# Attention and gated feed-forward on one core: constant copies moved in ScalarE's order, row maxima added first, a new list of steps

## The chip, the cores and the metric

The program runs on one core of a Trainium2 chip. The metric is the device time of one execution in microseconds (us), lower is better. The kernel before takes 883.32 us (median of 3 runs, 883.28 to 883.49).

## The reference

Eight batches, eight heads, 576 positions, head size 64. Heads 0 to 3 attend to the 32 nearest earlier positions; heads 4 to 7 to every fourth of the last 128. What comes out (4608 tokens of 512 numbers) goes through a gated feed-forward layer.

```python
scores = scale * np.matmul(q, k.transpose(0, 1, 3, 2))          # scale = 1/sqrt(64)
mask_plain = (rel >= 0) & (rel < 32)
mask_dil = (rel >= 0) & (rel < 128) & (rel % 4 == 0)
scores = np.where(masks[None], scores, -1e9)
scores = scores - np.max(scores, axis=-1, keepdims=True)
attn = np.exp(scores)
attn = attn / (np.sum(attn, axis=-1, keepdims=True) + 1e-09)
out = np.matmul(attn, v)                    # q: [8, 8, 576, 64]
x = out.transpose(0, 2, 1, 3).reshape(4608, 512)
h = x @ w_in                                # w_in: 512 x 2048
g = h * np.tanh(log1p(exp(h)))
return g @ w_out                            # w_out: 2048 x 512
```

## The kernel before, in words

The work is cut into 16 units, each half of a batch (288 tokens). Of each unit the attention is done for four pairs of heads, then the first product with `w_in` (`ff1`), the gate, and the second product with `w_out` (`ff2`). Every number is held as a high and a low 16-bit part, so a product with weights is three 16-bit products. Units 0 to 2 ("direct") do their attention in f32 and take the plain weights; from unit 4 on the first product is done with seven combined forms of the weights for two units at once.

The weights themselves are made on the chip, in pieces `(k, g, p)` (k = 0 for `w_in`, 1 for `w_out`; g a chunk of 512 columns, p a half of its rows). A piece goes through steps with names of two letters: `wl` loads it into one of four buffers `raw`, `wm` takes a magnitude on ScalarE (L392/L394), `ww` shifts that and joins it to the raw words on VectorE (L445, L447), `wa` takes absolute values on ScalarE (L399), `ws` sums magnitudes over partitions on TensorE (L413) and makes a scale on VectorE (L420 to L426), `wp` splits into a high part on ScalarE (L458) and a low part on VectorE (L461). The raw buffer is free for the next load after that.

Attention of a direct unit `u` and pair: `sp` puts mask and scores into a PSUM bank (L683: the identity copy `ident_b` times the mask copy `m_fb`; L686: q times k); `sc` takes the negated maximum of each row on VectorE (L716, into `nm`). Units 0 and 1 (`ACROSS`) then make the scores a second time, transposed, in `across` (step `tp`): masks, k times q, and `nm` times the identity in f32 are added up in one bank (three loops, all L819), and ScalarE takes the exponential from there (L839). Unit 2 transposes its probabilities instead (L800). `va` multiplies with the values (L853), `tx` transposes the result (L897 with `is_transpose`, L900) and takes away the high part (L915). `pr` makes the scale of a unit's values (magnitudes L350 on ScalarE, `largest`: L355 on TensorE, L358 and L360 on VectorE, L363 on TensorE).

All steps are generators. `ORDER`, a list of some 2,350 names that a planner wrote out, sets which generator is advanced next; `=n` behind a name gives the number of the buffer that the step takes. Each engine carries out its instructions in that order. `kwN` (`keep_warm`) issues N products of a 128x128 tile of zeros on TensorE (L1169); nobody reads what they give.

Three copies of constants on ScalarE stand outside the list: `m_fb` (L294), `ident_b` (L296), `minus` (L315). A scheduler places these; on ScalarE they stand behind the first `wm` (L392). The loads of a unit (`loads`, L475 to L496) are issued on SP's queue; those of unit 0 are in two parts, with a `yield` between.

Of the kernel before, what the change touches and what calls it, by code (L numbers as in the profile page):

```python
# [43 lines left out]
wl0.0.0=1 wm0.0.0=0 ww0.0.1 kw4=1 kw4=2 kw4=3 kw4=1 sp0.0=2 kw4=3 kw4=1 kw4=3 sc0.1 tp0.1=0 kw4=1 xa1.1=0 kw4=3
ww0.0.1 ww0.0.0 kw4=1 ww0.0.0 kw4=1 kw8=3 wa0.0.1 wa0.0.0 kw4=1 kw4=3 tp0.1=1 kw4=1 sc0.0 ws0.0=1 ws0.0 kw4=3 ld0
sp0.2=2 wl0.3.0=2 tp0.0=0 sc0.2 tp0.2=3 kw4=1 wm0.3.0=0 ww0.3.0 xa0.0=1 lv0 va0.1=2 ww0.3.0 pr0=0 kw12=1 wl0.3.1=3
kw4=1 wp0.0.1 xa2.1=2 pr0=1 wp0.0.1 pr0 lv1 tp0.0=0 ld1 wl0.2.0=0 tp0.2=1 sp0.3=0 sc0.3 xa1.0=3 wm0.3.1=0 pr0=3 pr0
ww0.3.1 kw4=1 va0.0=1 wp0.0.0 kw4=0 ww0.3.1 kw4=3 kw4=0 kw4=3 va0.1 tp0.3=0 va0.0 kw12=3 wa0.3.0 kw4=3 wa0.3.1 ws0.3=3
xa0.1=4 va0.0=0 kw4=1 tp0.3=0 va0.3=0 va0.3 wp0.0.0 wl0.2.1=1 va0.2=1 va0.1=2 ws0.3 wp0.3.0 tx0.0=3 va0.3=1 kw4=2
tx0.0 wp0.3.0 va0.2 wp0.3.1 sp1.1=0 va0.2=3 sp1.0=2 sc1.1 wp0.3.1 tx0.0 tx0.0 wm0.2.0=0 sc1.0 tx0.1=1 tx0.1 sp1.2=0  # L50
sc1.2 wm0.2.1=0 ww0.2.0 ww0.2.0 ww0.2.1 wl0.1.1=2 ww0.2.1 tp1.0=3 tx0.1 tx0.1 tp1.2=2 sp1.3=0 ff0.6=1 tp1.0=0 ff0.7=3
wa0.2.0 wm0.1.1=0 sc1.3 ww0.1.1 wa0.2.1 wl0.1.0=3 ws0.2=0 wm0.1.0=0 pr1=1 ff0.6 ww0.1.0 ws0.2 ws0.1=0 ff0.7 ws0.1
pr1=0 pr1 tp1.2=1 ff0.0=2 pr1=0 wp0.2.1 wp0.2.1 pr1 fs0 wp0.2.0 wp0.2.0 ff0.0 tp1.3=0 ff0.6=1 ww0.1.0 fs1 va1.0=1
ff0.0=2 ff0.7 wl1.2.0=1 va1.2=2 tp1.3=0 ff0.1=3 wl1.2.1=0 va1.3=0 ff0.1 va1.0 va1.2 ww0.1.1 va1.0=0 va1.2=2 tp1.1=1
wp0.1.0 wp0.1.0 wm1.2.0 ww1.2.0 wp0.1.1 wp0.1.1 tp1.1=0 ff0.4=2 va1.3 va1.3=3 ff0.4 tx1.1=1 wm1.2.1 ww1.2.1 ww1.2.1
va1.1=0 ld2 ff0.1 ff0.4=0 ws1.2=3 gt0.0=0 va1.1 ff0.5=2 wl1.3.1=3 ws1.2 va1.1=1 tx1.1 gt0.0 ww1.2.0 gt0.3=1 ff0.5
ff0.5 gt0.2=2 gt0.2 ff0.3=3 tx1.0=2 tx1.0 wm1.3.1 tx1.1 wp1.2.0 wp1.2.0 ff0.2=0 ff0.2 tx1.1 lv2 pr2 ff0.2=2 ff0.3
ff0.3 tx1.0 tx1.0 sp2.3=1 sp2.1=0 ff1.2=3 wl1.3.0=2 ff1.2 sc2.3=0 ff1.6=2 ff1.6 wm1.3.0 gt0.3 sc2.1=1 ww1.3.1 wp1.2.1
ex2.1 ww1.3.0 ex2.3 ff1.6=0 wp1.2.1 ww1.3.1 ws1.3=0 ww1.3.0 ws1.3 ff1.2=1 ff1.3=1 gt0.1=7 gt0.1 wl1.0.0=1 ff1.3 ff1.3
ff1.7=2 pr2=0 wm1.0.0 tp2.3=1 lv3 tp2.3=1 sp2.0=3 wp1.3.0 ff1.7 wl1.0.1=0 pr2 fo0.2.0=1 fo0.2.1 tp2.1=0 ff1.7 sp2.2=2  # L60
wf1.1=2 wm1.0.1 wp1.3.0 ww1.0.0 wp1.3.1 wf1.1 sc2.2=2 sc2.0=1 gt1.1=3 fo0.3.0 tp2.1=0 ex2.0 wl1.1.1=2 ex2.2 fo0.3.1
gt1.1 ff1.1=0 ff1.1 va2.1=3 ww1.0.1 fs2 va2.3=2 wp1.3.1 wl1.1.0=3 ww1.0.1 va2.1 va2.3 va2.1=0 va2.3=3 wf1.1=1 wf1.1
fo0.2.2 tp2.2=3 wm1.1.1 ww1.1.1 ws1.0=2 ws1.0 tp2.2=0 fo0.2.3 wf1.1 gt1.3=4 va2.2=3 va2.2 ff1.0=2 wm1.1.0 gt1.3 ff1.0
xa3.1=1 ff1.0=2 va2.2=1 ff1.1 gt1.0=5 ww1.1.0 fo0.3.2 fo0.3.3 fo0.3.3=0 fo0.2.3=1 fo0.3.3 ww1.1.0 tx2.1=3 tx2.1
tp2.0=2 tp2.0=1 ww1.1.1 ld3 wp1.0.1 ww1.0.0 wp1.0.0 ff1.5=0 ff1.5 wp1.0.1 ws1.1=1 ws1.1 ff1.4=2 tx2.1 tx2.1 wp1.1.1
ff1.4 ff1.4=0 va2.0=1 va2.0 wp1.1.0 wp1.0.0 fo0.0.0=3 fo0.0.1 fo0.0.2 gt1.0 fo1.2.0=2 fo1.2.1 wf0.0=1 ff1.5 wp1.1.1
fo0.2.3 fo1.3.0 fo0.0.3 va2.0=2 wp1.1.0 gt1.2=6 wf1.0=2 tx2.0=0 gt1.2 ol pr3 pr3 wf0.0 wf1.0 pr3 pr3=1 pr3 fo1.2.2
# [1162 lines left out]
```

## Time and profile before

| | |
|---|---|
| median of 3 runs | 883.32 us |
| the profiled execution | 883.64 us |
| its span | 881.9 us |
| TensorE (PE) busy | 867.8 us, 98% of the span |
| VectorE (DVE) busy | 668.4 us, 76% |
| ScalarE (ACT) busy | 676.0 us, 77% |
| products of zeros (L1169) | 208 |

The span runs from the first to the last instruction; the execution's own time is 1.74 us more. The page of the profile gives each engine's busy time over the whole span, and TensorE is busy nearly throughout. So the questions are in which stretches it is idle or slow, and which of its instructions need not be there. The views used are the busy times by stretch, with the clock that TensorE was granted (1.00 is 2.4 GHz, 0.50 is 1.2 GHz), the waits of TensorE, and the timelines of the first 130 us.

### The profile page before, as it was taken

Reading aid. Unit: us, or ns where it says so; the run is one execution under the profiler, and the core shown is the slowest. Engines: PE = TensorE matmul, PEld = TensorE weight load, DVE = VectorE, ACT = ScalarE, POOL = GpSimd, SP = SyncE. Lnnn points to the kernel's source line nnn. Section 1 sums busy time; section 2 is a strip of 40 time slices with the busy share of each in tenths; the row PEclk is TensorE's granted clock in tenths of the full one; section 3 lists DMA queues with packets and bytes.
Section 4 is the critical chain, followed back from the end, with each engine's and each line's share of the span. In section 5 each row is a group of like instructions: output and inputs, shape, how many; then the busy total and the mean of one; then the engine's idle time right before and its main releaser. Section 6 shows DMA issues by size and latency. Waiting matters only on the chain.

```text
span 881.9 us, 21715 instructions
## 1 busy us (share of the span) xinstructions
PE 867.8 (98%) x9076; PEld 700.9 (79%) x9079; DVE 668.4 (76%) x1034; ACT 676.0 (77%) x978; POOL 19.0 (2%) x93
## 2 busy tenths in 40 slices
...
GB/s 253 219 114 240 154 139 96 126 163 169 148 174 185 201 198 190 168 159 179 211 154 189 174 155 213 167 163 218 168 155 180 117 194 111 121 117 159 111 8 48
DMA packets 211010, 141.21 MB, mean 160 GB/s; under 512 B 151392, under 2 KB 195936, under 8 KB 210912
## 3 DMA queue, kind: packets, MB, share of 16 engines
...
## 4 chain that ended last, share of the span: by engine, by line
PE 65%; DVE 6%; ACT 4%; issue 1%; DMA 1%; DVEq 0%; ACTq 0%
PE b L1140 33%; PE b L1025 26%; PE b L859 3%; PE b L686 2%; DVE nm L716 1%; DVE sb L710 1%; DVE g L1130 1%; DMA w<-wd 1%; PE b L1113 1%; DVE p L790 1%; ACT sb L743 0%; ACT L743 0%; DVE hm L971 0%; DVE w L1010 0%; DVE g L1010 0%
## 5 line engine op out<-in xcount | busy, mean ns | idle before, releaser
L1140 PE MATMUL b<-g,w 128*128 128x288 f16 x3072 | 391.9, 286 | 1.2 <-DVE w L461 1.2
L1140 PEld LDWEIGHTS <-w 128*128 128x128 f16 x3072 | 296.4, 98 | 75.8 <-DVE w L461 1.4
L1025 PEld LDWEIGHTS <-w 128*128 128x128 f16 x2016 | 195.3, 98 | 50.0 <-DMA w<-wd 0.4
L1025 PE MATMUL b<-xf,w 128*128 128x288 f16 x1440 | 211.1, 286 | 0.1
L1130 DVE SCALAR_TENSOR_TENSOR g<-hm,sg,g 128x1152 f16<-128x1152 f32 x64 | 90.1, 1411 | 29.1 <-ACT g L1128 29.0
L1113 PE MATMUL b<-xf,w 128*128 128x288 f16 x768 | 99.6, 286 | 0.4 <-DVE y L1152 0.2
L1113 PEld LDWEIGHTS <-w 128*128 128x128 f16 x768 | 74.3, 98 | 20.0 <-issue 0.6
L1128 ACT ACTIVATE g<-hm,sg 128x1152 f16<-128x1152 f32 x64 | 80.0, 1252 | 1.1
L1154 ACT ACTIVATE y<-b,fo 128x288 f32<-128x288 f32 x60 | 42.7, 736 | 41.1 <-PE b L1140 41.1
L1035 ACT ACTIVATE hm<-hm,fs 128x576 f32<-128x576 f32 x72 | 54.1, 768 | 13.3 <-DVE hm L1086 8.6
L1025 PE MATMUL b<-w,w 128*128 128x288 f16 x288 | 63.4, 286 | 0.0
L743 ACT ACTIVATE sb<-sb,ln_p 96x768 f32<-96x768 f32 (+3 forms) x52 | 46.3, 897 | 9.0 <-DVE sb L718 8.8
L718 DVE TENSOR_TENSOR sb<-sb,nm 96x768 f32<-96x768 f32 (+4 forms) x64 | 49.2, 769 | 2.2
L716 DVE TENSOR_REDUCE nm<-sb 96x6 f32<-96x768 f32 (+4 forms) x64 | 48.8, 763 | 1.8
L790 DVE TENSOR_TENSOR p<-sb,p 96x768 f16<-96x768 f32 (+3 forms) x52 | 46.8, 904 | 2.9 <-ACT p L788 2.9
L1086 DVE TENSOR_TENSOR hm<-b,hm 128x576 f32<-128x576 f32 x24 | 18.1, 753 | 38.8 <-PE b L1025 33.8
...
L859 PEld LDWEIGHTS <-pT 128*128 128x128 f16 (+3 forms) x1092 | 38.5, 98 | 2.2
L1025 PE MATMUL b<-xg,w 128*128 128x288 f16 x288 | 39.2, 286 | 0.2 <-ACT hm L1042 0.2
L1010 DVE TENSOR_TENSOR w<-w,w 72x1024 f16<-72x1024 f32 (+3 forms) x31 | 29.6, 957 | 6.6 <-ACT w L1008 6.6
L686 PEld LDWEIGHTS <-q 64*72 64x72 f16 (+1 forms) x1092 | 27.8, 116 | 8.4 <-issue 8.1
L1008 ACT CAST w<-w 72x1024 f16<-72x1024 f32 (+3 forms) x31 | 25.8, 836 | 10.5 <-DVE w L999 2.7
...
## 6 DMA issues: line engine op xcount, KB each, us to landing
...
```

Source lines behind the costliest of these rows:

```text
L686: nc.tensor.matmul(o, q, k, start=start, stop=stop, skip_group_check=True)
L716: nc.vector.tensor_reduce(nm[:nq, :, j:j + n], x, axis=AX.X, op=ALU.max, negate=True)
L718: nc.vector.tensor_tensor(blocked(sb, c0, n, w), x, nm[:nq, :, j:j + n].unsqueeze(3).broadcast_to([nq, 2, n, w]), op=ALU.add)
L743: nc.scalar.activation(x, x, AF.Exp, bias=ln_p[:nq])
L790: nc.vector.tensor_tensor(lo, src, hi, op=ALU.subtract)
L859: nc.tensor.matmul(avv[:, h, j], pp[:nk, c:c + P], vv[vi][:nk, j, hh, :], start=(i == 0), stop=(i == 2))
L1025: nc.tensor.matmul(o[:, h, :HT], t[:, c, wi, h * P:(h + 1) * P], form_of(p, x, c, xi), skip_group_check=True, start=start and n == 0, stop ...
L1035: nc.scalar.activation(o, src, AF.Mish, scale=U[2 * p]["fs"][:, j:j + 1])
L1113: nc.tensor.matmul(ph[:, h, :HT], w1[j][c // WIDE][:, c % WIDE, wi, k * P:(k + 1) * P], x_of(d, xi, c), start=(n == 0), stop=(n == len(seq ...
L1128: nc.scalar.activation(g[:, 0], m, AF.Identity, scale=sg)
L1130: nc.vector.scalar_tensor_tensor(g[:, 1], m, sg, g[:, 0], ALU.mult, ALU.subtract)
L1140: nc.tensor.matmul(po[:, :HT], w2[:, e, j, wi, k * P:(k + 1) * P], d["g"][j][:, gi, k, :], start=(j == 0 and n == 0), stop=(j == NCH - 1 a ...
```

## The change

1. The three copies on ScalarE are issued at the head of the list, behind the first activation.
2. In `across` the product with `nm` comes first, with `is_transpose=True`; it opens the accumulation (`start`), and the last product of q and k closes it.
3. `ORDER` is another list: the same steps, each as often as before, in another order up to about a third of the list, then in the same order with a few other buffer numbers. The 45 `kw` entries with 208 products of zeros become 35 with 164. The loads of unit 0 are in two parts in both kernels; `loads` is not touched.

```diff
@@ constants
     m_fb = const.tile([QB, 2 * P + QB], BF16, name="m_fb")
-    nc.scalar.mul(m_fb, m_f, math.sqrt(D))
     ident_b = const.tile([QB, QB], BF16, name="ident_b")
-    nc.scalar.copy(ident_b, ident[:QB, :QB])
...
     minus = const.tile([P, P], F16, name="minus")
-    nc.scalar.mul(minus, ident, -1.0)
@@ across
+        for j, x in enumerate(bl):
+            for h in range(2):
+                mm(at(h, x), nm[:nq, h, j:j + 1].broadcast_to([nq, x[2]]), ident[:nq, :nq], is_transpose=True, start=j == 0,
+                   stop=False)
         for x in bl:
             for h in range(2):
-                mm(at(h, x), m_fb[:nq, col:col + x[2]], ident_b[:nq, :nq], start=x is bl[0], stop=False)
+                mm(at(h, x), m_fb[:nq, col:col + x[2]], ident_b[:nq, :nq], start=False, stop=False)
...
-                mm(at(h, x), kn[hs, k0:k0 + x[2]], d["qn"][hs, pair, x[1]:x[1] + nq], start=False, stop=False)
-        for j, x in enumerate(bl):
-            for h in range(2):
-                mm(at(h, x), nm[:nq, h, j:j + 1].broadcast_to([nq, x[2]]), ident[:nq, :nq], start=False, stop=x is bl[-1])
+                mm(at(h, x), kn[hs, k0:k0 + x[2]], d["qn"][hs, pair, x[1]:x[1] + nq], start=False, stop=x is bl[-1])
@@ the list is carried out
         nc.scalar.activation(first, ln_p, AF.Exp)
+        nc.scalar.copy(ident_b, ident[:QB, :QB])
+        nc.scalar.mul(m_fb, m_f, math.sqrt(D))
+        nc.scalar.mul(minus, ident, -1.0)
@@ ORDER
-kw4=0 kw8=1 kw4=0 kw4=2 kw4=3 kw4=0 kw4=2 kw4=1 kw4=3 kw8=0 kw4=1 kw4=2 kw4=3 ld0 sp0.1=0 wl0.0.1=0 wm0.0.1=0 kw4=1
...
+kw4=3 kw4=0 kw4=1 kw4=2 kw8=3 kw4=0 ld0 wl0.0.1=0 kw4=1 wm0.0.1=0 ww0.0.1 ww0.0.1 kw4=2 kw4=3 kw4=1 kw4=3 kw4=2 xa1.1=0 kw8=0 kw4=1 kw4=3 sp0.1=2 sp0.0=0
...
```

ScalarE at the start of the program, before (first fence) and after the change (second). `raw_76` and `raw_77` are the first two loaded pieces of `w_in`, `w_...` their places.

```order
L1179 ACT_TABLE_LOAD
L1179 ACTIVATE first<-ln_p 128x1
L392 ACTIVATE w_119<-raw_76 128x1024
L296 CAST ident_b<-ident 96x96
L315 ACTIVATE minus<-ident 128x128
L294 ACTIVATE m_fb<-m_f 96x352
L392 ACTIVATE w_118<-raw_77 128x1024
```

```order
L1177 ACT_TABLE_LOAD
L1177 ACTIVATE first<-ln_p 128x1
L1178 CAST ident_b<-ident 96x96
L1179 ACTIVATE m_fb<-m_f 96x352
L1180 ACTIVATE minus<-ident 128x128
L389 ACTIVATE w_116<-raw_76 128x1024
L389 ACTIVATE w_115<-raw_77 128x1024
```

The three copies have moved from behind the first magnitude, which reads a loaded piece, to ahead of it.

VectorE at the start of the program, before and after; `nm` are the row maxima of the first two pairs.

```order
L445 TENSOR_SCALAR w_119<-w_119 128x1024
L716 TENSOR_REDUCE nm<-b_72 96x2x2
L716 TENSOR_REDUCE nm<-b_72 96x2
L447 SCALAR_TENSOR_TENSOR raw_76<-raw_76,w_119 128x1024
L445 TENSOR_SCALAR w_118<-w_118 128x1024
L447 SCALAR_TENSOR_TENSOR raw_77<-raw_77,w_118 128x1024
L716 TENSOR_REDUCE nm<-b_74 96x2x2
```

```order
L442 TENSOR_SCALAR w_116<-w_116 128x1024
L444 SCALAR_TENSOR_TENSOR raw_76<-raw_76,w_116 128x1024
L713 TENSOR_REDUCE nm<-b_74 96x2x2
L713 TENSOR_REDUCE nm<-b_74 96x2
L442 TENSOR_SCALAR w_115<-w_115 128x1024
L444 SCALAR_TENSOR_TENSOR raw_77<-raw_77,w_115 128x1024
L713 TENSOR_REDUCE nm<-b_72 96x2x2
```

The joining of the first piece now stands ahead of the first row maxima.

TensorE at the first `across` (step `tp0.1`), before and after; rows that repeat are left out, x4 is a number of products.

```order
L1169 MATMUL b_75<-zeros 128x128
L819 LDWEIGHTS m_fb
L819 MATMUL b_72<-ident_b,m_fb 128x96
L819 MATMUL b_72<-ident_b,m_fb 96x96
L819 MATMUL b_72<-qn,knp 128x96 x4
L819 MATMUL b_72<-qn,knp 96x96 x2
L819 MATMUL b_72<-ident,nm 128x96 x4
L819 MATMUL b_72<-ident,nm 96x96 x2
```

```order
L1167 MATMUL b_75<-zeros 128x128
L816 MATMUL b_73<-ident,nm 128x96 x4
L816 MATMUL b_73<-ident,nm 96x96 x2
L816 LDWEIGHTS m_fb
L816 MATMUL b_73<-ident_b,m_fb 128x96
L816 MATMUL b_73<-ident_b,m_fb 96x96
L816 MATMUL b_73<-qn,knp 128x96 x4
L816 MATMUL b_73<-qn,knp 96x96 x2
```

The products with `nm` went from the end of the step to its head.

## Rows read from the trace of the kernel before

**Rows 1.** Busy time by stretch: stretch, its us, engines' busy us (instructions), PEclk, DMA share, GB/s.

```profile
1.05:6.06 5.01, 5.01 (x60) 4.83 (x60) 0.00 (x0) 1.17 (x2) 2.40 (x14) 1.00 0.77 206
6.06:11.33 5.27, 0.00 (x1) 0.12 (x1) 0.69 (x1) 1.87 (x4) 0.00 (x0) 0.97 0.99 365
11.33:17.50 6.17, 6.17 (x48) 4.96 (x47) 3.91 (x5) 2.27 (x2) 0.00 (x0) 0.50 1.08 309
17.50:53.97 36.47, 36.36 (x512) 31.87 (x513) 23.91 (x44) 24.40 (x33) 0.78 (x2) 1.00 0.72 210
53.97:143.20 89.23, 87.75 (x858) 72.44 (x857) 79.67 (x142) 74.36 (x119) 2.97 (x2) 1.00 0.52 159
143.20:299.00 155.80, 153.53 (x1694) 122.76 (x1694) 150.66 (x240) 135.19 (x198) 8.91 (x31) 1.00 0.64 151
299.00:870.00 571.00, 570.70 (x5854) 457.55 (x5849) 409.36 (x601) 434.50 (x622) 3.45 (x39) 1.00 0.63 158
```

**Rows 2.** TensorE's waits: who waited for whom, us in total, times, longest.

```profile
PE b L683 <- ACT m_fb L294: 5.3, 1, 5.3
PE b L355 <- ACT vdh L350: 1.7, 1, 1.7
PE b L1140 <- DVE w L461: 1.2, 1, 1.2
```

**Rows 3.** ScalarE's timeline: start us, us, line, operation, tiles, count, idle before.

```profile
9.40 1.12 ACT L392 ACTIVATE w<-raw 128x1024 f32<-128x1024 f32 x1 [7.18 <-DMA raw<-in_w_in]
10.79 0.48 ACT L294 ACTIVATE m_fb<-m_f 96x352 bf16<-96x352 f32 x1
11.87 1.12 ACT L392 ACTIVATE w<-raw 128x1024 f32<-128x1024 f32 x1 [0.60 <-DMA raw<-in_w_in]
15.66 1.15 ACT L399 ACTIVATE w<-raw 128x1024 bf16<-128x1024 f32 x1 [2.67 <-DVE raw L447]
23.67 1.06 ACT L350 ACTIVATE pp<-vdn 72x1024 bf16<-72x1024 f32 x1
```

**Rows 4.** VectorE's timeline, the first row maxima and the first pieces of weights.

```profile
10.56 0.69 DVE L445 TENSOR_SCALAR w<-w 128x1024 int32<-128x1024 int32 x1 [9.57 <-ACT w L392]
13.55 0.95 DVE L716 TENSOR_REDUCE nm<-b 96x4 f32<-96x512 f32 x2 [2.29 <-PE b L686]
14.42 1.21 DVE L447 SCALAR_TENSOR_TENSOR raw<-raw,w 128x1024 int32<-128x1024 int32 x1
17.80 0.95 DVE L716 TENSOR_REDUCE nm<-b 96x4 f32<-96x512 f32 x2 [0.31 <-PE b L686]
```

**Rows 5.** TensorE's timeline from the first scores to the first `ff1`.

```profile
11.33 0.75 PE L683 MATMUL b<-m_fb,ident_b 96*96 96x352 bf16 x2 [5.27 <-ACT m_fb L294]
12.01 1.49 PE L686 MATMUL b<-knp,qn 64*96 64x128 f32 x12
...
18.43 0.43 PE L819 MATMUL b<-ident_b,m_fb 96*128 96x96 bf16 x6
18.79 0.86 PE L819 MATMUL b<-qn,knp 64*128 64x96 f32 x12
19.58 1.47 PE L819 MATMUL b<-ident,nm 96*128 96x96 f32 x12
20.88 2.17 PE L1169 MATMUL b<-zeros 128*128 128x128 f16 x36
22.89 1.03 PE L413 MATMUL b<-w,ones 128*128 128x512 bf16 x3
...
28.50 1.26 PE L819 MATMUL b<-ident,nm 72*72 72x72 f32 x16
...
38.15 1.03 PE L413 MATMUL b<-w,ones 128*128 128x512 bf16 x3
...
47.86 1.58 PE L819 MATMUL b<-ident,nm 96*128 96x96 f32 x12
...
51.13 1.68 PE L819 MATMUL b<-ident,nm 72*104 72x72 f32 x16
...
53.97 3.11 PE L1113 MATMUL b<-xf,w 128*128 128x288 f16 x24
```

**Rows 6.** TensorE's timeline, transposes of 96x96 (six) and 72x72 (eight) tiles.

```profile
86.17 0.66 PE L897 MATMUL b<-ident,xs 96*128 96x96 f32 x6
105.69 0.69 PE L800 MATMUL b<-ident,sb 72*72 72x72 f32 x8
```

**Rows 7.** VectorE's timeline, L421 early and while GpSimd clears buffers.

```profile
24.68 0.15 DVE L421 TENSOR_SCALAR wf<-wm 128x1 int32<-128x1 int32 x1
...
139.18 1.25 DVE L421 TENSOR_SCALAR wf<-wm 128x4 int32<-128x4 int32 x1
```

More of the change, by code (lines that the diff above doesn't have):

```diff
@@ L42 @@
 ORDER = """
-kw4=0 kw8=1 kw4=0 kw4=2 kw4=3 kw4=0 kw4=2 kw4=1 kw4=3 kw8=0 kw4=1 kw4=2 kw4=3 ld0 sp0.1=0 wl0.0.1=0 wm0.0.1=0 kw4=1
[L44 to L67, printed above, removed]
@@ new lines @@
+xa1.1=0 kw8=0 kw4=1 kw4=3 sp0.1=2 sp0.0=0 kw4=1 sc0.1 kw4=3 kw4=1 wl0.0.0=1 wm0.0.0=0 ww0.0.0 kw4=3 ww0.0.0 kw4=1
+kw8=3 tp0.1=1 ld0 sp0.2=3 wa0.0.1 kw4=2 wl0.3.0=2 kw4=2 wa0.0.0 lv0 wm0.3.0=0 sc0.0 ws0.0=0 kw4=2 wl0.3.1=3 sc0.2
+tp0.2=3 tp0.1=0 pr0=1 ws0.0 kw4=2 va0.1=0 ww0.3.0 ww0.3.0 tp0.0=1 wp0.0.1 wp0.0.1 tp0.0=0 tp0.2=1 kw8=2 sp0.3=2 kw4=1
+pr0=1 kw8=3 wa0.3.0 kw4=3 xa0.0=1 pr0 pr0=1 wm0.3.1=0 va0.0=3 sc0.3 kw4=2 lv1 pr0 kw4=1 ww0.3.1 va0.1 wp0.0.0 ww0.3.1
+ld1 tp0.3=2 wp0.0.0 va0.0 kw4=1 wa0.3.1 kw8=1 ws0.3=1 tp0.3=0 va0.0=0 va0.1=2 va0.3=2 tx0.0=0 ws0.3 xa0.1=2 va0.3
@@ new lines @@
+wp0.3.0 va0.2=1 kw4=3 wl0.2.0=0 kw4=3 va0.2 tx0.0 sp1.1=3 tx0.0 va0.3=0 wp0.3.1 wp0.3.0 va0.2=1 sp1.0=2 sc1.1 tx0.1=1
+sp1.2=3 sc1.0 tp1.0=2 tx0.0 wp0.3.1 wl0.2.1=1 wm0.2.0=0 sc1.2 tx0.1 ww0.2.0 ww0.2.0 wm0.2.1=0 tx0.1 tx0.1 ww0.2.1
+wl0.1.1=2 wa0.2.0 ww0.2.1 tp1.0=1 wa0.2.1 wm0.1.1=0 wl0.1.0=3 tp1.2=0 lv2 sp1.3=3 wm0.1.0=0 sc1.3 ff0.6=1 xa1.0=3
+ws0.2=2 ws0.2 ww0.1.0 ff0.7=3 ff0.7 pr1=0 ww0.1.1 ws0.1=2 ff0.6 tp1.2=0 ws0.1 pr1=0 pr1 ff0.0=2 wp0.2.0 wp0.2.1 pr1=0
+wp0.2.0 ff0.0 pr1 fs0 ff0.6=0 ff0.7 va1.2=0 ff0.0=1 va1.0=1 wl1.2.0=0 va1.0 va1.2 wp0.2.1 tp1.3=3 tp1.3=1 ff0.1=2
@@ new lines @@
+ww0.1.1 wp0.1.1 va1.0=1 wl1.2.1=1 va1.2=3 ww0.1.0 wm1.2.0 wp0.1.1 tp1.1=3 ww1.2.0 tp1.1=0 wp0.1.0 wp0.1.0 ld2 va1.3=1
+ff0.1 va1.3 va1.1=0 fs1 wm1.2.1 ff0.4=3 va1.3=2 ff0.4 va1.1 wl1.3.1=2 ff0.1 gt0.3=4 ww1.2.1 ff0.4=2 va1.1=0 ws1.2=1
+tx1.0=0 ww1.2.1 tx1.0 ws1.2 tx1.1=2 ff0.5=3 ww1.2.0 gt0.3 ff0.5 tx1.1 tx1.1 gt0.0=3 tx1.0 wl1.3.0=3 pr2 ff0.2=1 ff0.5
+tx1.1 ff0.2 ff0.3=3 xa3.0=4 ff0.3 wp1.2.0 wp1.2.0 tx1.0 wp1.2.1 wp1.2.1 sp2.3=2 wm1.3.0 ww1.3.0 gt0.0 sp2.1=0 ff0.2=0
+ff0.3 wl1.0.0=0 sc2.3=0 sc2.1=1 wm1.3.1 gt0.2=0 ff1.2=1 ff1.6=3 ff1.6 ex2.3 ff1.2 ww1.3.1 ws1.3=2 wl1.1.1=1 ww1.3.0
@@ new lines @@
+ex2.1 ff1.7=0 ff1.7 gt0.2 ff1.2=1 ff1.6=2 ws1.3 gt0.1=2 wp1.3.0 tp2.3=2 ww1.3.1 sp2.2=1 ff1.7 wp1.3.0 ff1.3=3 gt0.1
+sc2.2=3 ff1.3 tp2.3=1 wf1.1=0 xa2.1=1 pr2=0 pr2 wm1.0.0 ww1.0.0 wf1.1 fo0.2.0=2 wm1.1.1 ww1.1.1 fo0.2.1 sp2.0=0 ff1.3
+ex2.2 fo0.2.2 sc2.0=2 wl1.0.1=3 wm1.0.1 wp1.3.1 ww1.0.1 tp2.1=3 tp2.1=0 fo0.3.0 va2.3=1 ex2.0 wp1.3.1 ww1.0.1 fo0.3.1
+tp2.2=3 gt1.1=1 gt1.1 tp2.2=1 va2.1=0 ws1.0=3 va2.1 va2.3 va2.1=1 fo0.3.2 gt1.3=5 fo0.3.3 fo0.3.3=1 ws1.0 wp1.0.1
+wf1.1=1 ww1.0.0 va2.2=0 va2.2 fo0.2.3 ld3 ff1.0=3 ff1.0 gt1.3 wl1.1.0=2 wm1.1.0 va2.3=0 ff1.1=1 va2.2=3 ff1.0=2 fs2
@@ new lines @@
+ww1.1.0 wp1.0.0 ws1.1=0 tx2.1=3 ff1.1 fo0.2.3=0 ww1.1.1 ww1.1.0 tx2.1 xa2.0=2 ws1.1 ff1.1 gt1.0=6 ff1.5=2 tx2.1 wf1.1
+tx2.1 ff1.4=1 ff1.4 wp1.0.0 fo0.0.0=0 tp2.0=3 wp1.1.1 wp1.1.0 tp2.0=1 wp1.1.1 wp1.1.0 wf1.1 ff1.5 va2.0=3 ff1.4=0
+ff1.5 gt1.2=7 gt1.0 lv3 wp1.0.1 fo0.0.1 fo0.0.2 wf0.0=2 gt1.2 va2.0 fo0.0.3 va2.0=3 tx2.0=2 ol pr3 pr3 fo0.2.3
+fo1.2.0=1 fo1.2.1 wf1.0=0 pr3 pr3=3 wf0.0 fo0.0.3=0 mr fo0.3.3 wf1.0 fo0.0.3 fo1.2.2 pr3 pr3=3 wf0.0=1 wf0.0 pr3
+fo1.2.3 pr3 fo0.1.0 xw3.0=1 wf0.1=2 pr3 pr3 wf0.0 fo1.2.3=1 fo1.2.3 pr3 pr3 ld4 fo0.1.1 fo0.1.2 fo0.1.3 pr3 tx2.0
@@ new lines @@
+zc2.0 tp6.1=0 za2.1=2 za2.1=2 zl2.6=2 zb2.1=3 zl2.7=0 tp6.1 tp6.2 zb2.1=0 fo3.1.3=0 zd2.1 zc2.1 zg2.1 zl2.8=1 va6.0=1
+pr7 tp6.1=0 gt4.0=1 gt4.0 zd2.1 zg2.1 pr7 pr7 ze2.1 ze2.1 za2.2=3 va6.0 zf2.1 zc2.2=0 pr7 pr7 zc2.1 za2.2=1 zc2.2
+zf2.1 gt4.1=2 va6.0 pr7 gt4.1 zb2.2=2 zb2.2=2 sp7.0=0 va6.1=1 sc7.0=3 va6.1 zl2.9=2 va6.1 zd2.2 zg2.2 zd2.2 ze2.2
+zl2.10=0 ze2.2 zc2.2 za2.3=0 ze2.1 tp6.3=0 tp6.3 zg2.2 zg2.1 gt5.1=5 gt5.1 zf2.2 zf2.2 sp7.1=1 zl2.11=1 tp6.2=1
+zc2.3=2 za2.3=0 zc2.3 gt4.2=4 gt4.2 zl2.12=2 zg2.2 zb2.3=3 sc7.1=0 zd2.3 sp7.2=2 sc7.2=2 zl2.13=0 ze2.2 zt3.0.0=0
```

223 lines of the change are left out of this document (109 added, 114 removed).

## The prediction

> **What bounds the kernel now.** The busy times by stretch come first. From 17.5 us to 870 us TensorE is idle for only 0.11 + 1.48 + 2.27 + 0.30 = 4.2 us [rows 1], so time can come only from its own instructions, its clock, or the stretch before. That stretch is poor: 5.27 us of idle, then 6.17 us at the granted clock 0.50, which is 1.2 GHz [rows 1]. The waits name the cause of the idle: the first mask product waits 5.3 us for `m_fb` [rows 2]. ScalarE's timeline shows why `m_fb` is late: it stands behind the magnitude of the first piece of weights, which starts at 9.40 when the load lands [rows 3]. VectorE is the second engine to watch: from 143.2 to 299 us it is busy 150.66 of 155.80 us [rows 1], so a lead of TensorE can't be spent there freely.
>
> **1. The copies of constants.** In the new order they wait for no load, only for the mask that GpSimd builds, and GpSimd's work is over by 6.06 [rows 1]; so they end far ahead of 9.40. The last of them ended at 11.27 before, so the second magnitude could be thought to start sooner; it doesn't, because it waited for its load until 11.87 anyway [rows 3]. The order on SP's queue is unchanged through the loads of unit 1, so I let the loads land when they did.
>
> What then starts the chain? The list puts the shift and the joining of the first piece ahead of the first row maxima on VectorE. From 9.40: magnitude 1.12 [rows 3], shift 0.69, joining 1.21, maxima 0.95 [rows 4], together 13.4 us. TensorE is there earlier: 68 zeros instead of 60 end at about 6.5, two pairs of scores cost 2.2 us each even at the low clock [rows 5], and 28 zeros cost 1.6. That is 12.6 at worst, and near 10.5 at the full clock if q and k have landed. These were issued ahead of the piece that landed at 9.40, so they take the start at most to 9.4 + 2.2 + 1.6 = 13.2. Either way `tp0.1` starts at 13.4 instead of 18.43 [rows 5]: **5.0 us gained**. The half-clock stretch is inside this number.
>
> The change adds a wait here: the product with `nm` now leads its step, so masks and q-times-k products, 0.43 + 0.86 us [rows 5], queue behind it, and ScalarE's exponential behind those. Before, they ran while VectorE finished: maxima ready at 18.75, needed at 19.58 [rows 4, 5]. In `tp0.1` this wait is in the 13.4; in the later steps the maxima are earlier in the order, and I price it at nothing. If that cover went, it would be up to 1.2 us a step.
>
> **2. From `tp0.1` to the first `ff1`.** Before, this took 53.97 - 18.43 = 35.54 us [rows 5], with 0.11 idle. Three terms change it.
> - *Zeros*: 112 stood here, 68 do now. At 36 in 22.89 - 20.88 = 2.01 us one costs 0.056 [rows 5]; 44 fewer are **2.5 us**.
> - *Row maxima as transposes*: six products in f32 show as 12 instructions of together 1.47 us; six transposes of the same size show as 6, and take 0.66 [rows 5, 6]. The forms here: two steps of 96 rows in unit 0 (1.47 - 0.66 = 0.81 each), two of 72 rows (1.26 - 0.69 = 0.57 each), and in unit 1 `tp1.0` (1.58 - 0.66 = 0.92) and `tp1.2` (1.68 - 0.69 = 0.99). Together **4.7 us**.
> - *New waits*: TensorE alone would now need 35.54 - 0.11 - 2.5 - 4.7 = 28.2 us and be at `ff1` at 41.6. VectorE has some 24 us of work in the old stretch [rows 1] and would have to do it in 28, so it will end last now and then. Following the order with the durations above I find two places. The small product behind `pr0` comes about 0.7 us after TensorE, since VectorE first splits the first piece. The weight sum of chunk 3 (at 38.15 before) waits for ScalarE's absolute values of its second piece, which wait for shift and joining, 0.69 + 1.21 + 1.15 [rows 3, 4]; I get 29.8 against TensorE at 29.1. I take **1.6 us lost** as an estimate. Bounds: 0, and 4.5 if the values of unit 0 land only when ScalarE read them before, at 23.67 [rows 3]; I count on about 21.
>
> So `ff1` starts at 43.2 instead of 53.97.
>
> **3. After the first `ff1`.** Two more `across` steps, `tp1.1` and `tp1.3`: 0.92 + 0.99; four zeros: 0.2. Together **2.1 us**. All other TensorE work is the same, in another order up to some 300 us and in the old order after. Its 4.05 us of idle there [rows 1] I leave as they are, which is the nearest row. Bounds: all of it gone, or 5 us more, since VectorE's own idle in the dense stretch is 5.1 us and TensorE's lead could be lost there. Other buffer numbers in the last two thirds I price at nothing: that stretch has 0.30 us of idle in 571 [rows 1].
>
> **The sum.** 5.0 + 0.1 + 2.5 + 4.7 - 1.6 + 2.1 = 12.8. From the profiled execution's 883.64 that is 870.8; the median of the runs lies 0.3 below it, so **870.5 us**.
>
> A rule bears on the second term. Rows show the transposes at 0.66 of 1.47, a factor of 0.45. The Trainium skill, "TensorE: Matmul & The Clock Gate" (Terms), gives the transpose mode as four times faster for FP32. By that the eight steps would save about 8 us where the rows give 6.6, and the time would be 869. The rows are the same operation in the same program, and decide.
>
> **Rivals.**
> - *The hand-over is rebuilt worse.* Between units 1 and 3 TensorE already waits 1.7 us for magnitudes and 1.2 us for a split [rows 2], and VectorE is slow there while GpSimd clears buffers: the same small operation took 1.25 us there and 0.15 at another time [rows 7]. If the new list lays these clearings on other VectorE work, some 5 us come on top: 875.5. For it: VectorE's 97% in that stretch. Against it: the engine's work up to each weight split is nearly the same in both lists.
> - *The clock falls in the wait before `tp0.1`.* If q and k land early, TensorE idles up to 2.9 us there. The clock fell during the 5.27 us of idle at 6.06, and did not in the waits of 1.7 and 1.2 us [rows 1, 2]; this one lies between. It came back after 6.17 us of work [rows 1]. Half of that is 3.1 us: 873.5.
> - *The start gains nothing*, because loads, not `m_fb`, hold the first scores until 11.33. Then the copies don't do what they are moved for, and 5.0 us are missing: 875.5. Against it: after `m_fb` the scores followed without any wait [rows 5].
> - *Slower: the clock stays low through the heads of unit 0.* With 44 zeros fewer and 112 product instructions turned into 56 transposes, TensorE might stay at 0.50 from 13.4 to the first `ff1`. That adds up to 28 us: near 898. It decides once the low clock lasts for some 25 us, since half of that eats the 12.8. Against it: 48 products, spaced by no more than their own length, brought the clock back in 6.17 us [rows 1], and the new stretch has as dense a stream. The Trainium skill, "TensorE: Matmul & The Clock Gate" (Part 4), says that transposes don't count towards the full clock as products do; no run here shows it, as the longest row of transposes is 0.69 us between products [rows 6].
>
> **How the numbers follow.** A measurement of this kernel can tell about 0.2% (1.8 us) from no change: under 881.5 is faster, over 885.1 slower. Forecast 0.63, worse hand-over 0.14, clock in the wait 0.11, no gain at the start 0.06, low clock throughout 0.04, and 0.02 for gains eaten up to nothing. All but the last two are faster: 0.94; same 0.02; slower 0.04. The range: from 870.5 down by the 4.05 us of idle and half of the waits, 866; up by the worse hand-over and most of the waits' bound, 878. It takes in the second to fourth cases.
>
> **What would show it.** Right, if in the new profile the first mask product starts before 9.4 us without a wait for `m_fb`; if the first transposes of `nm` start near 13.4, in groups of 6 and 8 at 0.66 and 0.69 us; if the first `ff1` starts at 43 (42 to 46); if TensorE is busy some 855 us; and if the stretch behind it, up to the end, is some 826 us long. Wrong, if TensorE's idle between 43 and 290 us is over 8 us, if the granted clock is 0.50 behind 13.4, or if `nm` still shows two instructions for a product.

## The result, and the profile after

The changed kernel takes **870.15 us** (median of 4 runs, 868.49 to 870.64) against 883.40 us for the kernel before (median of 4 runs, 883.28 to 884.84). The ratio is 0.9843, with a 95% interval from 0.9826 to 0.9860: 13.25 us less, where 12.8 were forecast. The profiled execution took 870.22 us; its span is 868.4 us, 13.5 less than before. TensorE is busy for 858.3 us of it (99%).

Busy time of the changed kernel by stretch, columns as in [rows 1]. The stretches end where TensorE's work changes: zeros; first scores; the wait ahead of `tp0.1`; up to the first `ff1`; and then up to the same distance from the end as in [rows 1].

```profile
1.05:6.79 5.74, 5.74 (x68) 5.74 (x69) 0.00 (x0) 2.02 (x5) 2.38 (x13) 1.00 0.81 228
6.79:10.92 4.13, 4.12 (x59) 3.23 (x56) 0.00 (x0) 1.12 (x1) 0.00 (x0) 1.00 0.98 366
10.92:13.67 2.75, 0.00 (x1) 0.03 (x1) 2.67 (x4) 1.39 (x3) 0.00 (x0) 1.00 1.14 332
13.67:44.82 31.15, 30.66 (x419) 25.50 (x421) 25.57 (x47) 23.73 (x33) 0.67 (x3) 0.95 0.93 277
44.82:138.98 94.16, 94.03 (x915) 77.22 (x915) 87.62 (x156) 86.00 (x136) 8.27 (x7) 1.00 0.47 146
138.98:290.00 151.02, 148.88 (x1648) 118.42 (x1646) 144.18 (x233) 128.69 (x188) 3.23 (x26) 1.00 0.69 168
290.00:856.50 566.50, 566.50 (x5813) 454.35 (x5811) 405.16 (x595) 430.82 (x615) 3.46 (x39) 1.00 0.64 158
```

The idle of 5.27 us and the 6.17 us at half clock ahead of `tp0.1` [rows 1] are gone; one wait of 2.75 us is left, in which VectorE is busy for 2.67. Behind the first `ff1` the idle is 0.13 + 2.14 us, where it was 4.05.

TensorE's timeline of the changed kernel, start, duration, work, and idle before it; it answers to [rows 5, 6].

```profile
6.79 0.46 PE L680 MATMUL b<-m_fb,ident_b 96*96 96x352 bf16 x2
7.19 0.85 PE L683 MATMUL b<-knp,qn 64*96 64x128 f32 x12
...
13.67 0.68 PE L816 MATMUL b<-ident,nm 96*128 96x96 f32 x6 [2.76 <-DVE nm L713]
14.19 0.42 PE L816 MATMUL b<-ident_b,m_fb 96*128 96x96 bf16 x6
...
19.45 0.67 PE L816 MATMUL b<-ident,nm 72*72 72x72 f32 x8
...
30.48 0.38 PE L410 MATMUL b<-w,ones 128*128 128x512 bf16 x1
31.03 0.59 PE L410 MATMUL b<-w,ones 128*128 128x512 bf16 x2 [0.17 <-ACT w L396]
...
44.82 1.64 PE L1111 MATMUL b<-xf,w 128*128 128x288 f16 x12
```

The first mask product starts at 6.79 instead of 11.33 and waits for nothing. `tp0.1` starts at 13.67 instead of 18.43, and the products with `nm` are now six rows in 0.68 us and eight in 0.67, where twelve took 1.47 and sixteen 1.26. The second weight sum starts at 30.48 instead of 38.15, the first `ff1` at 44.82 instead of 53.97.

ScalarE's timeline of the changed kernel, beside [rows 3]:

```profile
3.01 0.50 ACT L1179 ACTIVATE m_fb<-m_f 96x352 bf16<-96x352 f32 x1 [0.62 <-POOL m_f L292]
...
9.80 1.14 ACT L389 ACTIVATE w<-raw 128x1024 f32<-128x1024 f32 x1 [6.09 <-DMA raw<-in_w_in]
```

And VectorE's, beside [rows 4]:

```profile
10.97 0.69 DVE L442 TENSOR_SCALAR w<-w 128x1024 int32<-128x1024 int32 x1 [9.98 <-ACT w L389]
11.70 1.23 DVE L444 SCALAR_TENSOR_TENSOR raw<-raw,w 128x1024 int32<-128x1024 int32 x1
12.84 0.95 DVE L713 TENSOR_REDUCE nm<-b 96x4 f32<-96x512 f32 x2
```

This is the forecast's chain from the landing of the first piece to the row maxima, link by link: 9.80, 10.97, 11.70, 12.84. The piece landed 0.4 us later than before, and the chain ended that much later.

TensorE's waits in the changed kernel, beside [rows 2]:

```profile
PE b L816 <- DVE nm L713: 2.8, 1, 2.8
...
PE b L360 <- ACT hm L1114: 0.9, 1, 0.9
PE b L1138 <- DVE g L1128: 0.5, 1, 0.5
PE b L857 <- DVE xs L875: 0.5, 1, 0.5
```

The three waits of [rows 2] (5.3, 1.7 and 1.2 us) are all gone. The last three here lie behind the first `ff1`.

One thing stood among the rivals of the forecast but not in its sum: the clock. The changed kernel's busy time around the wait, the eighth column the granted clock (1.00 is 2.4 GHz, 0.50 is 1.2 GHz):

```profile
13.67:15.30 1.63, 1.63 (x24) 1.51 (x24) 1.59 (x3) 0.80 (x1) 0.00 (x0) 1.00 0.95 319
15.30:15.60 0.30, 0.30 (x6) 0.16 (x2) 0.30 (x2) 0.00 (x0) 0.00 (x0) 0.66 1.14 342
15.60:18.60 3.00, 2.96 (x27) 2.18 (x27) 1.67 (x4) 2.49 (x4) 0.00 (x0) 0.50 0.87 198
18.60:30.00 11.40, 11.12 (x178) 10.02 (x178) 8.11 (x19) 8.64 (x15) 0.52 (x1) 0.99 0.90 239
```

The clock is full through the wait and for the first 1.7 us of work after it; then it is at 1.2 GHz for about 3 us. Half of that, some 1.5 us by estimate, is lost.

Where the 13.5 us of the span come from, by these rows: up to `tp0.1` 18.43 - 13.67 = 4.76; from there to `ff1` 35.54 - 31.15 = 4.39; behind it (881.9 - 53.97) - (868.4 - 44.82) = 4.35.

### The profile page after: what moved, and what is told of

Its sections match the earlier page's. It is cut to its first block, busy times and chain, and to the rows that moved or that the text cites. A ratio compares the mean times of both kernels' runs of the same rounds, so it can differ in the third digit from the quotient of the medians.

```text
span 868.4 us, 21528 instructions
## 1 busy us (share of the span) xinstructions
PE 858.3 (99%) x8976; PEld 691.0 (80%) x8979; DVE 665.4 (77%) x1034; ACT 676.0 (78%) x978; POOL 18.5 (2%) x93
## 4 chain that ended last, share of the span: by engine, by line
PE 70%; DVE 5%; ACT 1%; issue 1%; DMA 0%; SPq 0%; DVEq 0%; ACTq 0%
PE b L1138 35%; PE b L1023 29%; PE b L857 3%; PE b L683 3%; DVE g L1128 1%; DVE p L787 1%; DVE sb L707 0%; DVE nm L713 0%; DMA out_T<-y 0%; DVE hm L969 0%; PE b L1111 0%; DVE sb L715 0%; ACT L1114 0%; ACT hm L1114 0%; DVE g L1008 0%
```

## Experiments

Each was timed in five rounds beside the kernel before, whose median in the three sessions was 883.78, 883.79 and 883.25 us. All of them compute the whole result; only order, form, and products of zeros, which nobody reads, differ.

**The two parts that can be done alone, in the old list.** `c1_copies` is the kernel before with the copies at the head of the list.

```diff
-    nc.scalar.mul(m_fb, m_f, math.sqrt(D))
-    nc.scalar.copy(ident_b, ident[:QB, :QB])
-    nc.scalar.mul(minus, ident, -1.0)
...
         nc.scalar.activation(first, ln_p, AF.Exp)
+        nc.scalar.copy(ident_b, ident[:QB, :QB])
+        nc.scalar.mul(m_fb, m_f, math.sqrt(D))
+        nc.scalar.mul(minus, ident, -1.0)
```

> The kernel before, with the three copies of constants at the head of ScalarE's work and nothing else. Theory A (the terms of the prediction add up, TensorE is the bound): the 5.3 us wait for the mask copy is gone, the first mask product starts before 7 us, the first weight sum about 5 us earlier than 22.9, and the time is 877 to 879.5. Theory B (the new list of steps is what gains; without it the lead of TensorE is lost again in waits for VectorE and ScalarE): 881 to 883.4.

Measured: 880.06 us (879.51 to 881.39), ratio 0.9964 (0.9951 to 0.9976): 3.7 us gained, less than the 5.0 of the forecast and more than nothing. TensorE's timeline of this kernel shows where the rest went:

```profile
12.55 0.42 PE L816 MATMUL b<-ident_b,m_fb 96*128 96x96 bf16 x6 [2.53 <-DVE nm L713]
...
13.69 2.38 PE L816 MATMUL b<-ident,nm 96*128 96x96 f32 x12
15.86 2.93 PE L1166 MATMUL b<-zeros 128*128 128x128 f16 x36
18.63 1.03 PE L410 MATMUL b<-w,ones 128*128 128x512 bf16 x4
```

`tp0.1` starts 5.9 us earlier than before, but its products with `nm` take 2.38 us instead of 1.47, and the 36 zeros 2.93 instead of 2.17: the granted clock is 0.51 from 14.0 to 17.5 us. The weight sum is only 4.3 us earlier (18.63 for 22.89), and so is `ff1` (49.69 for 53.97). So the low clock of [rows 1] isn't removed with the wait for `m_fb`; a shorter piece of it comes behind the new wait.

`c2_transposes` is the kernel before with the changed `across` (the second block of the diff, nothing else).

> The kernel before, with the row maxima of across added first and as transposes, and nothing else. Theory A: eight steps save 6.6 us of TensorE's work and lose about 0.3 us at the first step, where the maxima are ready after the masks: 876 to 878.5. Theory B: the saving is hidden behind waits: 880 to 883.4.

Measured: 876.76 us (875.30 to 877.50), ratio 0.9921 (0.9908 to 0.9933): 7.0 us gained, forecast 4.7 + 1.9 = 6.6 for this part. The wait for `m_fb` is still there (4.2 us, 1.0 less than before), and TensorE's timeline has the new form at the new price:

```profile
17.14 0.66 PE L819 MATMUL b<-ident,nm 96*128 96x96 f32 x6
```

Not all of the 7.0 is the form. By the spans 881.9 - 874.5 = 7.4 us are gained, of which 18.43 - 17.14 = 1.29 lie ahead of `tp0.1`, where no product was changed. From there to `ff1` (48.80) it is 3.88, with a new wait of 0.67 us for row maxima in unit 1, and behind it 2.23: together 6.1.

`c3_both` has both edits in the old list, with its 208 zeros.

> The kernel before with both edits, on the old list of steps with its 208 products of zeros. Theory A: the two gains add up to some 11.5 us, 871 to 873.5, so that the new list is worth 1 to 3 us. Theory B: 876 or more, so that the new list is worth most.

Measured: 873.43 us (872.03 to 873.96), ratio 0.9882 (0.9869 to 0.9896), 10.35 us gained; the two alone give 3.72 + 7.02 = 10.74, so they add up within the spread of the runs. The changed kernel is another 3.3 us faster, and that is the new list. By the spans, 45.86 - 44.82 = 1.04 us of it lie ahead of `ff1`, and 825.64 - 823.58 = 2.06 behind. TensorE's waits behind `ff1` in this kernel:

```profile
PE b L352 <- ACT vdh L347: 1.7, 1, 1.7
PE b L1138 <- DVE w L458: 1.2, 1, 1.2
```

These are the two late waits of [rows 2], still there with both edits in, and gone in the changed kernel. The list takes them away.

**The two parts taken out of the changed kernel.** `c4_plain_maxima` is the changed kernel with the old form of `across`.

```diff
...
+                mm(at(h, x), m_fb[:nq, col:col + x[2]], ident_b[:nq, :nq], start=x is bl[0], stop=False)
...
+        for j, x in enumerate(bl):
+            for h in range(2):
+                mm(at(h, x), nm[:nq, h, j:j + 1].broadcast_to([nq, x[2]]), ident[:nq, :nq], start=False, stop=x is bl[-1])
```

> The changed kernel, with the row maxima last and as plain f32 products again. Theory A: the 6.6 us come back, less about 1.2 us at the first step, where masks and scores fill the wait again: 875 to 877. Theory B: 870.5 to 872.

Measured: 874.85 us (873.27 to 875.53), ratio 0.9898 (0.9883 to 0.9914): 4.7 us slower than the changed kernel, somewhat less than the 7.0 that the form gave in the old list. TensorE's timeline of this kernel tells why:

```profile
10.90 0.42 PE L816 MATMUL b<-ident_b,m_fb 96*128 96x96 bf16 x6
11.26 0.86 PE L816 MATMUL b<-qn,knp 64*128 64x96 f32 x12
13.21 1.44 PE L816 MATMUL b<-ident,nm 96*128 96x96 f32 x12 [1.09 <-DVE nm L713]
```

With `nm` last, masks and scores run while VectorE finishes the maxima, the wait is 1.09 us instead of 2.76, and in this execution the clock doesn't fall. With `nm` first, they queue behind it. So the new form pays for its 6.6 us with 2 to 3 us at the start: 6.6 - 4.7 by the medians, and by the profiled executions 4.7 - 1.67, since `ff1` starts at 46.49 here. This is the wait that the forecast named as added, and the clock that follows it.

`c5_copies_late` is the changed kernel with the copies behind the first magnitude again.

```diff
...
+            if name == "wm0.0.1":
+                nc.scalar.copy(ident_b, ident[:QB, :QB])
+                nc.scalar.mul(m_fb, m_f, math.sqrt(D))
+                nc.scalar.mul(minus, ident, -1.0)
```

> The changed kernel, with the three copies behind the first magnitude on ScalarE, where they stood before. Theory A: the first mask product waits until about 11.3 us again, the granted clock is 0.50 behind that wait, and the first across step starts 2 to 4 us later than 13.7: 872.5 to 875. Theory B (in the new list the start hangs on VectorE's joining of the first piece alone, so that the copies matter little): 870 to 871.5.

Measured: 873.38 us (872.16 to 873.84), ratio 0.9882 (0.9868 to 0.9895): 3.2 us slower. TensorE's timeline has the wait for `m_fb` back, and `tp0.1` at 17.84:

```profile
11.17 0.74 PE L680 MATMUL b<-m_fb,ident_b 96*96 96x352 bf16 x2 [3.34 <-ACT m_fb L1191]
...
17.84 0.66 PE L816 MATMUL b<-ident,nm 96*128 96x96 f32 x6
```

`tp0.1` is 4.2 us later, `ff1` (47.43) only 2.6: here the low clock lies ahead of `tp0.1` (11.2 to 17 us), and the stretch behind it takes 29.6 us instead of 31.15. That is the same 1.6 us as in `c1_copies`, from the other side.

**What the zeros cost.** `z1_no_zeros_behind` leaves out the 68 zeros between `tp0.1` and `ff1`.

```diff
-kw8=3 tp0.1=1 ld0 sp0.2=3 wa0.0.1 kw4=2 wl0.3.0=2 kw4=2 wa0.0.0 lv0
+kw8=3 tp0.1=1 ld0 sp0.2=3 wa0.0.1 wl0.3.0=2 wa0.0.0 lv0
...
```

> The changed kernel without the 68 products of zeros that stand behind the first across step. Theory P (as the prediction counted them: each costs TensorE 0.056 us on the path): 3.8 us less, about 866.4. Theory W (they stand in gaps that are there anyway, and fewer of them is a sign of shorter waits and not their cause): 869 to 870.5, and TensorE's idle up to the first ff1 grows by 2.5 us or more.

Measured: 870.35 us (869.64 to 874.57), ratio 0.9862 (0.9841 to 0.9882), no faster than the changed kernel. At 0.056 us each [rows 5] 3.8 us of work are gone. The busy time of the stretch and TensorE's waits in this kernel:

```profile
13.72:43.63 29.91, 25.67 (x350) 20.93 (x352) 25.77 (x47) 25.00 (x33) 0.27 (x3) 1.00 0.94 292
```

```profile
PE b L410 <- ACT w L396: 3.1, 2, 1.7
...
PE b L360 <- DVE dg L357: 0.7, 1, 0.7
```

Idle grew from 0.49 to 4.24 us, by 3.75, just what the zeros took. They filled waits for ScalarE's absolute values and for VectorE. The stretch is 1.24 us shorter than in the changed kernel, but at the granted clock 1.00 instead of 0.95; a clock that low cost 1.6 us in `c1_copies`, so nothing is left for the zeros. The single runs agree: two runs here with a mean granted clock of 0.998 took 869.85 and 870.35 us, three of the changed kernel with the same clock 870.09 to 870.64. Two other runs here have 0.996 and 0.992 and took 872.76 and 874.57; whether the missing zeros lowered the clock there isn't shown, as neither was the profiled one.

`z3_no_zeros_ahead` leaves out the 28 zeros ahead of `tp0.1` instead.

```diff
-sp0.0=0 kw4=1 sc0.1 kw4=3 kw4=1 wl0.0.0=1 wm0.0.0=0 ww0.0.0 kw4=3 ww0.0.0 kw4=1 kw8=3 tp0.1=1
+sp0.0=0 sc0.1 wl0.0.0=1 wm0.0.0=0 ww0.0.0 ww0.0.0 tp0.1=1
```

> The changed kernel without the 28 zeros ahead of the first across step: the wait there grows from 2.76 to 4.4 us and nothing else changes. If the wait lowers the clock, the granted clock falls to 0.50 in every execution and earlier, and the time rises by 0.5 to 3 us, 870.7 to 873. If the clock doesn't matter there: 870 to 870.5.

Measured: 872.81 us (870.85 to 873.41), ratio 0.9877 (0.9860 to 0.9893), 2.7 us more by the medians, with an interval that just touches that of the changed kernel. Busy time of this kernel in the wait, which is now 4.9 us long, and behind it:

```profile
11.00:13.92 2.92, 0.00 (x0) 0.03 (x1) 2.66 (x4) 1.53 (x3) 0.00 (x0) 0.59 1.11 341
13.92:18.00 4.08, 4.08 (x33) 3.38 (x34) 2.81 (x5) 2.77 (x3) 0.00 (x0) 0.50 0.94 263
```

The clock falls inside the wait and stays at 0.50 until about 21 us. So the zeros ahead of the wait have an effect, though they hold up nothing: they shorten the idle time, and the low clock with it.

**The wait filled.** `z2_zeros_in_wait` puts 48 more zeros into it.

```diff
-kw8=3 tp0.1=1
+kw8=3 kw48=3 tp0.1=1
```

> The changed kernel with 48 more products of zeros (2.7 us) in the wait of 2.76 us ahead of the first across step. If that wait is what lets the clock fall to 0.50 at 15.7 us, the granted clock stays at 1.00, the weight sum at 17.9 starts about 1 us earlier, and the time is 868 to 869. If something else lowers it (the transposes that follow), the clock falls as before and the time is 870 to 871.

Measured: 870.20 us (868.62 to 874.86), ratio 0.9854 (0.9832 to 0.9877), the same as the changed kernel. The profiled execution was the slowest (874.86). Its busy time around `tp0.1`, a row of ScalarE's timeline, and what follows from it on TensorE:

```profile
13.40:15.30 1.90, 1.90 (x26) 1.65 (x26) 1.87 (x4) 0.91 (x1) 0.00 (x0) 1.00 1.00 353
15.60:18.60 3.00, 2.95 (x49) 2.41 (x48) 2.24 (x6) 2.58 (x4) 0.00 (x0) 1.00 0.85 191
```

```profile
40.11 1.12 ACT L389 ACTIVATE w<-raw 128x1024 f32<-128x1024 f32 x1 [3.97 <-DMA raw<-in_w_in]
```

```profile
42.61 0.67 PE L913 MATMUL b<-xf,minus 128*128 128x288 f16 x2 [2.64 <-ACT xf L906]
46.00:48.00 2.00, 2.00 (x19) 1.62 (x19) 0.23 (x1) 2.00 (x4) 0.00 (x0) 0.50 0.36 84
```

Around `tp0.1` the clock stays full, so the fall there is owed to the idle time. But the time isn't won: TensorE was ahead by some 1.4 us at the second weight sum (29.04 for 30.48), and ScalarE then waited 3.97 us for the fifth piece of `w_in`. That kept TensorE waiting for 2.64 us, and 2.1 us after it had gone on the clock fell after all: it is at 0.50 from about 44.7 to 51.5 us. The wait and, by estimate, half of these 6.8 us are more than enough to make this execution the slowest. It doesn't stand for the others: four runs took 868.62 to 870.46 us at a mean clock of 0.999 or 1.000, where this one has 0.996. Nor is the fifth piece late whenever TensorE is early: in `z1_no_zeros_behind` the last two products of the second weight sum start as early (29.83 us, and 29.85 here), and ScalarE waits 0.52 us for this piece. Why a full clock brought the four runs so little stays open.

**Four attempts at a faster version.** `o1_maxima_first` takes the row maxima of the first two pairs ahead of the first piece's weight work, so that `tp0.1` waits less.

```diff
-wm0.0.1=0 ww0.0.1 ww0.0.1 ... sc0.1 ... sc0.0
+sc0.1 sc0.0 wm0.0.1=0 ww0.0.1 ww0.0.1
```

> The changed kernel with the row maxima of the first two pairs ahead of the shift and joining of the first piece on VectorE. The first across step starts at about 10.9 instead of 13.67, and TensorE's wait moves behind it, to the first weight sum. Theory A: the sum hangs on the second piece's load (landed at 12.3) and starts 1 us earlier, TensorE has done more by then, and the next waits are shorter: 868 to 869.5. Rival: only the place of the wait changes: 869.8 to 870.5.

Measured: 871.48 us (870.25 to 874.59), ratio 0.9858 (0.9843 to 0.9873). `tp0.1` starts at 11.21, but the wait has moved behind it: the first weight sum waits 1.73 us for ScalarE. And the clock does worse; that wait, and the busy time behind it:

```profile
16.87 0.58 PE L410 MATMUL b<-w,ones 128*128 128x512 bf16 x1 [1.73 <-ACT w L396]
16.30:30.00 13.70, 12.90 (x109) 10.97 (x110) 4.47 (x9) 8.26 (x14) 0.00 (x0) 0.50 0.88 227
```

`p1_values_late` moves the values of unit 1 (`lv1`) behind the load of the fifth piece on SP's queue.

```diff
-sc0.3 kw4=2 lv1 pr0 kw4=1 ... wl0.2.0=0 kw4=3
+sc0.3 kw4=2 pr0 kw4=1 ... wl0.2.0=0 lv1 kw4=3
```

> The changed kernel, with the loads of unit 1's values (7 us of issuing on SP's queue) moved behind the load of the fifth piece of w_in. In the run with zeros in the wait, ScalarE waited 4.0 us for that piece. Theory: the piece is on time in every run, so the spread of the runs shrinks, and the median is 868.5 to 870. Rival: the load was late in that one execution only; 870 to 870.5, with the same spread.

Measured: 872.48 us (870.16 to 872.69), ratio 0.9871 (0.9854 to 0.9888), no gain. SP's queue, ScalarE's timeline and a stretch of busy time in this kernel:

```profile
19.28 0.43 SPq L482 DMA_DIRECT2D qn<-in_qT  x1
25.46 0.60 SPq L484 DMA_DIRECT2D knp<-in_kT  x1
...
28.33 2.25 SPq L511 DMA_DIRECT2D vn<-in_v  x3
30.63 5.77 SPq L513 DMA_DIRECT2D vdn<-in_vd  x4
36.50 6.06 SPq L372 DMA_DIRECT2D raw<-in_w_in  x6
```

```profile
43.91 1.14 ACT L389 ACTIVATE w<-raw 128x1024 f32<-128x1024 f32 x1 [2.72 <-DMA raw<-in_w_in]
```

```profile
14.00:18.00 4.00, 4.00 (x42) 3.18 (x40) 2.42 (x5) 2.46 (x3) 0.00 (x0) 0.52 0.89 221
```

The values occupy SP for 8.0 us here and for 6.8 in the changed kernel (19.24 to 26.13). There they cost the queue little: here, without them, it waits 5.7 us until 25.46, for TensorE (L816) to be done with the buffer of the next keys. Moved, they hold up the sixth piece, and ScalarE waits 2.72 us for it. But TensorE waits nowhere for more than 0.4 us on that account, so this isn't what makes `ff1` 1.63 us later (46.45). The clock accounts for it: the wait ahead of `tp0.1` is 3.25 us in this execution, and behind it the clock is at 0.50 from 14.2 to 21.0 us, some 3.4 us longer than in the changed kernel, of which half would be 1.7. Most of this lies ahead of the place where the values were moved from. The one run with a mean clock of 0.998, as the changed kernel mostly has it, took 870.16 us; the other three have 0.996 and 0.997.

`p2_values_late_zeros` is this with the 48 zeros of `z2_zeros_in_wait`; `p3_maxima_first_zeros` is the order of `o1_maxima_first` with `lv1` late and 42 zeros behind `sp0.2`.

> Both edits together: 48 zeros in the wait ahead of the first across step, and the values of unit 1 loaded later. If the clock in the wait and the late piece were the two things that kept the start from being shorter, both are away, the first ff1 starts at about 43.5, and the time is 867.5 to 869. If the start hangs on VectorE and ScalarE alone: 869.5 to 870.5.

> The row maxima first on VectorE as in the earlier run, now with 42 zeros in the wait that this moves behind the third pair's scores, and with the values of unit 1 loaded later. If the low clock from 16.3 to 30 us was what cost the earlier run its gain, the granted clock stays at 1.00 and the time is 867.5 to 869. If the order on VectorE is worse in itself: 870 to 871.5.

Measured: 871.40 us (869.46 to 875.67), ratio 0.9871 (0.9849 to 0.9894), and 871.78 us (871.38 to 875.22), ratio 0.9884 (0.9864 to 0.9905). In both profiled executions the clock stayed full through the start, and ScalarE waits 2.46 and 4.00 us for the sixth piece. In the second of them this reaches TensorE, which waits 1.37 us for ScalarE right ahead of `ff1`. In the first it doesn't (0.31 us at most); there the first piece landed at 10.71 us instead of 9.80, and `tp0.1` (14.59) and `ff1` (45.43) are later with it. The medians of all four attempts lie above what either of their theories allowed, and none is faster than the changed kernel.

## Why the prediction was right, and where its steps were off

The time (870.15 for 870.5) and the cause were right: the copies out of the load's way, and the products with `nm` as transposes, carry most of it. The sum is better than its terms. Of the signs named, the first mask product (6.79), the transposes (13.67, in groups of 6 and 8) and `ff1` (44.82) came as said; TensorE is busy for 858.3 us, not some 855, and the stretch behind `ff1` is 823.6 long, not 826. One sign of being wrong came too: the granted clock is 0.50 behind 13.4, from 15.6 to 18.6 us.

| part | forecast | measured |
|---|---|---|
| copies | 5.0 | 3.7 alone (`c1_copies`), 3.2 when undone (`c5_copies_late`) |
| transposes | 4.7 + 1.9 | 7.0 alone (`c2_transposes`; 6.1 by stretches), 4.7 when undone (`c4_plain_maxima`) |
| list: zeros 2.5 + 0.2, idle 0.1, waits -1.6 | 1.2 | 3.3 (changed kernel against `c3_both`) |

- **The start.** The start of `tp0.1` moved by 4.76 us where 5.0 were forecast. The failed step is the sentence that the half-clock stretch is inside this number. About 3 us of it come back behind the wait and cost 1.2 us (31.15 against 29.91 in `z1_no_zeros_behind`, if its missing zeros cost nothing) to 1.6 us (against 29.59 in `c5_copies_late`). Of the rival "the clock falls in the wait" the event happened and the price was half of the 3.1: three of the four runs of the changed kernel have a mean granted clock of 0.998 and took 870.1 to 870.6 us, one has 1.000 and took 868.5. In `c3_both` and `c4_plain_maxima` too the runs at 1.000 are faster than those at 0.998, by 1.3 and 1.4 us in the mean. That the difference between these runs is the clock is likely but not shown: the run of `c1_copies` at 1.000 took 880.06 us, amid the four at 0.998 (879.51 to 881.39), and `z2_zeros_in_wait` kept the clock in four of five runs and was no faster.
- **The transposes.** Six of 96 take 0.68 and 0.66 us, eight of 72 0.67, as the rows of other transposes said [rows 6]. The Trainium skill, "TensorE: Matmul & The Clock Gate" (Terms), puts the mode at four times faster for FP32; the trace disagrees once more, with 0.68 of 1.47. By that factor the eight steps would save three quarters of their 11.98 us, which is 9.0 and not the prediction's 8, and the time would be 868. Part 4 of that page of the Trainium skill says that transposes don't count towards the full clock; the rival beside it (near 898 us) did not come, and in `z2_zeros_in_wait` the clock was 1.00 from 13.4 to 44.6 us with the same transposes amid other products. The added wait was priced at nothing in the later steps: that holds for the new list, while on the old one `tp1.0` waits 0.67 and 0.65 us for its maxima (`c2_transposes`, `c3_both`).
- **The zeros.** The count was wrong: between `tp0.1` and `ff1` stood 104 zeros, not 112, and behind `ff1` 12, not 4, so the two terms should be 36 zeros or 2.0 us, and 0.7; their sum stays. That fewer zeros ahead of `ff1` give time was wrong as a cause. `z1_no_zeros_behind` takes out 68 and gains nothing. Up to `ff1` the net of the list came near (2.5 + 0.1 - 1.6 = 1.0 forecast, 0.5 with the right count, 1.04 measured), but only because the zeros' price and the waits' price were two sides of one thing: zeros stand where a wait would be.
- **Behind `ff1`.** 2.1 us were forecast and 4.35 came. The transposes alone brought (881.9 - 53.97) - (874.5 - 48.80) = 2.2 in `c2_transposes`. TensorE's work behind `ff1` shrank by 820.30 - 817.77 = 2.53, which is the transposes' 1.91 and the 12 zeros. The rest is the idle that the forecast left as it was: it fell from 4.05 to 2.27 us, inside the bounds named. The rival of a worse hand-over is refuted; VectorE is busy for 144.18 of 151.02 us there, no fuller than before.

So three errors nearly cancel by the spans: the start was 0.2 and the stretch up to `ff1` 1.3 us too good, the tail 2.25 too poor; together 0.7, which is 12.8 against 13.5. That the sum fits this well is luck.
